# Decode attention of two blocks on one core: the first load, block A's wq, as eight loads of 16 rows

## The chip, the core and the metric

The kernel runs on one core of a Trainium2 chip. The metric is device time in microseconds (us) of one execution. Before the change the median of three runs is 1937.3 us (1937.21 to 1937.73). One further execution was taken with the hardware profiler; its page and trace are what is read here.

## What is computed

Two blocks, A and B, each one decoding step of attention: a batch of 2, one query position, 32 heads of 192, a cache of 8192 positions. A projects x with wq to a query for each head, takes the softmax of its products with the cached keys, sums the cached values by it and projects with wo; B does the same with its own data. All data is bfloat16.

```
def _A_ref(x, k_cache, v_cache, wq, wo):
    q = (x @ wq).reshape(B, Sq, Hq, Dh).transpose(0, 2, 1, 3)
    scores = jnp.einsum("bhqd,bhkd->bhqk", q, k) * (Dh ** -0.5)
    p = _softmax(scores, axis=-1)
    o = jnp.einsum("bhqk,bhkd->bhqd", p, v)
    return o.transpose(0, 2, 1, 3).reshape(B, Sq, Hq * Dh) @ wo
...
return jnp.concatenate([a, b], axis=-1)
```

The caches are 4 x 201 MB, each wq and wo 7.9 MB (640 x 6144 and 6144 x 640). Every byte is read once.

## The kernel before

**Units.** The work is cut into 64 units: 2 blocks x 16 pairs of heads x 2 batch entries. A unit has one k load and one v load, each 128 rows (partitions) of 24576 elements: two heads, 64 rows to a head. Three buffers of that size (`NBUF` = 3) lie in one large tile, `big`; loads take them in turn. Block A's wq and block B's wq (128 rows of 30720 elements each, `WQE`) lie at first where buffers 1 and 2 and the product tiles will be.

**Engines.** For a unit, VectorE (DVE) multiplies k by the query in four chunks (L285), TensorE (PE) sums the products over groups of elements with an identity matrix (L362), DVE reduces these to scores (L289) and takes the maximum, GpSimd (POOL) spreads the maximum over all partitions (L266), ScalarE (ACT) takes the exponential (L324), and PE multiplies it with v (L376). The result is divided by its sum and kept in `qall` for the last projection.

**The prologue.** PE waits for x (the semaphore `("x",)`), transposes it (`pe_x`, L345), and DVE spreads it over partitions (L271). Then PE waits for block A's wq, and makes the queries of block A's 16 pairs (L354); then it waits for block B's wq, and makes those of block B. DVE (L275) and ACT (L280) copy them into `qall`. The first product L285 waits for all of them.

**Loads.** All are issued on one queue, by the SyncE engine (SP), in an order written out by hand (L480 to L492): wq A, x A, x B, wq B, then k and v of all units, then wo A, and wo B in five pieces of 29, 11, 5, 2 and 1 rows of wo for each partition, and the two stores of the output. A k or v load waits before its issue for the work that last read its buffer (`done`); the second and third of them wait for the queries of block A and of block B. wq A is issued ahead of the stream's list and has no wait.

**Semaphores of loads.** Each load adds 16 to a semaphore when it is complete. `dsem(k, n)` makes one for key `k`, and whoever waits for the key waits for 16 times `n`. The two loads of x share one with `n` = 2.

**The tail.** PE multiplies the collected outputs with wo, 96 products for each block (L404); block B's start when its first piece has landed. ACT and DVE copy the result out of the accumulator, and SP stores it.

Of the kernel before, what the change touches and what calls it, by code (L numbers as in the profile page):

```python
# [117 lines left out]
def build_kernel(nc, blocks, out):  # L118
# [28 lines left out]
    with ExitStack() as es:  # L147
# [7 lines left out]
        big = sb("big", [128, NBUF * BUFE + 2 * PRODE], BF16)  # L155
# [28 lines left out]
        WQE = DC * Hn * Dh  # L184
        wq_off = [BUFE, BUFE + WQE]
# [10 lines left out]
        S_act = _Stream("act", sem("s_act"), reg)  # L196
        S_dve = _Stream("dve", sem("s_dve"), reg)
        S_pool = _Stream("pool", sem("s_pool"), reg)
        bsem = [sem(f"bsem{i}") for i in range(NBUF)]

        def dsem(k, n=1):
            reg[k] = (sem("d_" + "_".join(str(i) for i in k)), 16 * n)

        dsem(("x",), NBLK)
        for blk in range(NBLK):
            dsem(("wq", blk))
            dsem(("odone", blk))

        loads = [("k", 0)]
# [14 lines left out]
        for blk, rows, off, w in ((0, (WR,), woA, [("s", LASTU, NCH - 1)]), (1, (29,), wo0, [("pv", LASTU - 1)]),  # L224
                                  (1, (11, 5, 2, 1), wo1, [("pv", LASTU)])):
            r = 29 if off == wo1 else 0
            for n in rows:
                pieces.append((blk, r, r + n, off, w))
                off, r, w = off + n * D, r + n, []
# [13 lines left out]
        def dma(out_ap, in_ap, k):  # L243
            s = reg[k][0]
            return lambda eng: eng.dma_start(out_ap, in_ap).then_inc(s, 16)  # L245
# [1 line left out]
        def ld_x(blk):  # L247
            return dma(x4[B * blk:B * blk + B, :], blocks[blk]["x"][:, 0, :], ("x",))

        def ld_wq(blk):  # L250
            src = blocks[blk]["wq"].rearrange("(j c) n -> j (c n)", c=DC)
            return dma(big[:, wq_off[blk]:wq_off[blk] + WQE], src, ("wq", blk))

        def ld_wo(n):
            blk, r0, r1, off, _ = pieces[n]
# [218 lines left out]
        def done(i):  # L474
# [2 lines left out]
            kind, u = loads[i]  # L477
            return ("m", u, NCH - 1) if kind == "k" else ("pv", u)

        ld_wq(0)(nc.sync)  # L480
        for blk in range(NBLK):
            S_sp.add(ld_x(blk))
        S_sp.add(ld_wq(1))
        for i, (kind, u) in enumerate(loads):
            w = [done(i - NBUF)]
# [73 lines left out]
def bass_concat_heads__gqa_block_cached__mha_block_cached__decode_kernel(  # L559
    nc: bass.Bass,  # L560
    A_x: bass.AP,
    A_k_cache: bass.AP,
    A_v_cache: bass.AP,
    A_wq: bass.AP,
    A_wo: bass.AP,
    B_x: bass.AP,
    B_k_cache: bass.AP,
    B_v_cache: bass.AP,
    B_wq: bass.AP,
    B_wo: bass.AP,  # L570
    out: bass.AP,
):
    blocks = [
        dict(x=A_x, k=A_k_cache, v=A_v_cache, wq=A_wq, wo=A_wo),
        dict(x=B_x, k=B_k_cache, v=B_v_cache, wq=B_wq, wo=B_wo),
    ]
    build_kernel(nc, blocks, out)
# [28 lines left out]
```

## Time and profile before

| what | value |
|---|---|
| median of three runs | 1937.3 us (1937.21 to 1937.73) |
| the profiled execution's own time | 1937.8 us |
| its span, first to last instruction | 1936.3 us |
| PE, DVE, ACT, POOL busy | 1506.7, 1122.1, 143.1, 28.6 us |
| mean granted PE clock | 0.953 |
| read from device memory | 836.77 MB, 432 GB/s over the span |
| wq A, from issue to landing | 20.9 us |
| wq B, from issue to landing | 37.9 us |
| a k or v load, from issue to landing (median) | 27.6 to 29.3 us |
| PE's first wait, for x | until 21.41 us |
| PE's last 96 products (L404, block B) | start at 1926.17 us |

The times of the page count from the first instruction. Engines: SP's queue is named SPq, and a line of the timeline gives start, duration, engine, line, operation and the tile written and read. A row of the windows' view gives a stretch, its length, the busy time of PE, PE's weight loads, DVE, ACT and POOL (with the number of instructions that start in it), the granted PE clock, the mean busy share of the 16 transfer engines, and the rate. Packets of a transfer are counted in the stretch in which they start.

### The profile page before, as it was taken

How to read it: one execution, taken by the hardware profiler on the slowest of the kernel's cores; microseconds unless marked ns; L12 is line 12 of the kernel's file. 1: busy time of each engine (PE TensorE's matmuls, PEld its weight loads, DVE VectorE, ACT ScalarE, POOL GpSimd, SP SyncE). 2: the span in 40 equal slices, each digit the busy share in tenths (PEclk: the TensorE clock that was granted, in tenths of full speed). 3: DMA queues.
4: the chain of work that ended last, by engine and by line, in shares of the span. 5: the costliest groups of instructions: out<-in, count | busy, mean ns of one | idle time of the engine just before them, and what ended most of it. 6: DMA issues, size and time to landing. Idle time of an engine off the chain costs nothing.

```text
span 1936.3 us, 19044 instructions
## 1 busy us (share of the span) xinstructions
PE 1506.7 (78%) x7721; PEld 731.1 (38%) x7721; DVE 1122.1 (58%) x907; ACT 143.1 (7%) x519; POOL 28.6 (1%) x113
## 2 busy tenths in 40 slices
PE   4777877877877877877877877877878878878878
PEld 2333433333433333433333433433334434434434
DVE  4765565565565565565565565565565565565560
ACT  3100000000000000000000000000000000000000
POOL 0000000000000000000000000000000000000000
PEclk9899999999999999999999999999988988988988
DMA  9999999999999999999999999999999999999999
GB/s 419 428 433 439 431 434 436 433 434 434 438 431 433 438 431 435 435 435 432 435 438 431 434 436 434 432 435 439 430 434 437 432 434 435 436 431 435 438 430 388
DMA packets 19610, 836.91 MB, mean 432 GB/s; under 512 B 2184, under 2 KB 2320, under 8 KB 2576
## 3 DMA queue, kind: packets, MB, share of 16 engines
q1 hardware_dynamic: 19600, 836.78, 99.9%
q8 instruction: 6, 0.10, 0.0%
q14 instruction: 4, 0.03, 0.0%
HBM read 836.77 MB, written 0.01 MB: 432 GB/s over the span
## 4 chain that ended last, share of the span: by engine, by line
DMA 49%; PE 31%; DVE 16%; issue 3%; DVEq 0%; SPq 0%; ACT 0%; ACTq 0%
DMA big<-in_B_k_cache_dram 24%; DMA big<-in_A_k_cache_dram 22%; PE ops L376 17%; DVE big L285 15%; PE scps L362 12%; DMA big<-in_B_wq_dram 2%; DMA big<-in_B_wo_dram 1%; DVE sc L289 1%; PE scps L354 0%; PE scps L404 0%; PE ops L368 0%; PE outps L354 0%; DVEq L285 0%; DVE qall L275 0%; SPq L245 0%
## 5 line engine op out<-in xcount | busy, mean ns | idle before, releaser
L285 DVE TENSOR_TENSOR big<-big,qall 128x6144 bf16<-128x6144 bf16 x256 | 853.0, 3352 | 519.6 <-DMA big<-in_B_k_cache_dram 259.8
L362 PE MATMUL scps<-big,ident 128*128 128x512 bf16 x3072 | 778.4, 410 | 395.8 <-DVE big L285 393.5
L376 PE MATMUL ops<-big,pb 128*34 128x384 bf16 x4096 | 676.8, 326 | 0.0
L362 PEld LDWEIGHTS scps<-big,ident 128*128 128x128 bf16 x3072 | 302.4, 104 | 865.1 <-DVE big L285 486.1
L376 PEld LDWEIGHTS ops<-big,pb 128*34 128x34 bf16 x4096 | 395.5, 98 | 258.7
L289 DVE TENSOR_REDUCE sc<-scps 128x32 f32<-128x512 f32 x256 | 176.2, 688 | 201.2 <-PE scps L362 201.2
L315 ACT ACTIVATE nb<-mg 64x1 f32<-64x1 f32 x128 | 25.9, 202 | 1707.6 <-POOL mg L266 1706.8
L324 ACT ACTIVATE pb<-sc,nb 64x128 bf16<-64x128 f32 x128 | 56.1, 438 | 7.8
L266 POOL PARTITION_ALL_REDUCE mg<-mp x64 | 25.9, 404 | 1859.2 <-DVE mp L295 1859.2
L295 DVE TENSOR_REDUCE mp<-sc 64x1 f32<-64x128 f32 x128 | 35.9, 280 | 8.3
L309 ACT ACTIVATE qall<-o_sum,rc 2x192 f32 (+1 forms) x64 | 29.2, 456 | 20.6 <-DVE o_sum L306 19.1
L306 DVE TENSOR_TENSOR o_sum<-ops,o_hi 2x192 f32<-2x192 f32 x64 | 22.1, 346 | 7.7
L354 PE MATMUL scps<-big,xw 128*128 x120 | 23.2, 351 | 2.8 <-DVE xw L271 2.2
L324 ACT ACTIVATION_READ_ACCUMULATOR pb<-sc,nb 64x1 f32 x128 | 23.9, 187 | 0.0
L303 DVE COPY o_hi<-ops 2x192 f32<-2x192 f32 x64 | 22.3, 348 | 2.0
L300 DVE RECIPROCAL rc<-ops 2x1 f32<-2x1 f32 x64 | 9.9, 155 | 21.3 <-PE ops L376 19.4
L275 DVE CAST qall<-scps 64x192 f32 x48 | 17.0, 355 | 7.3 <-PE scps L354 5.6
L280 ACT ACTIVATE qall<-scps 64x192 f32 x48 | 15.7, 326 | 30.5 <-DVE qall L275 28.3
L345 PE MATMUL oTps<-ident,xw 4*128 4x4 bf16 x5 | 0.4, 178 | 21.4 <-DMA xw<-in_B_x_dram 21.4
L354 PEld LDWEIGHTS scps<-big,xw 128*128 128x128 bf16 x120 | 12.4, 103 | 12.2 <-issue 6.1
L368 PEld LDWEIGHTS ops<-ones,rs 128*2 128x2 f32 x128 | 5.5, 82 | 26.9 <-issue 26.9
L271 DVE CAST xw<-oTps 128x320 bf16<-128x320 f32 x4 | 1.7, 484 | 18.5 <-PE oTps L345 18.5
(34 smaller groups left out, 74.0 us busy)
## 6 DMA issues: line engine op xcount, KB each, us to landing
big<-in_A_k_cache_dram SPq DMA_DIRECT2D x32, 6144.0 KB, 29.3
big<-in_A_v_cache_dram SPq DMA_DIRECT2D x32, 6144.0 KB, 28.3
big<-in_B_k_cache_dram SPq DMA_DIRECT2D x32, 6144.0 KB, 28.6
big<-in_B_v_cache_dram SPq DMA_DIRECT2D x32, 6144.0 KB, 27.6
big<-in_A_wq_dram SPq DMA_DIRECT2D x1, 7680.0 KB, 20.9
big<-in_B_wq_dram SPq DMA_DIRECT2D x1, 7680.0 KB, 37.9
big<-in_A_wo_dram SPq DMA_DIRECT2D x1, 7680.0 KB, 28.7
big<-in_B_wo_dram SPq DMA_DIRECT2D x1, 4640.0 KB, 29.0
```

The lines of the kernel that those rows point to most:

```text
L266: return lambda eng: eng.partition_all_reduce(mg[u % 3][:], mp[u % 3][:], 128, bass.bass_isa.ReduceOp.max)
L285: return lambda eng: eng.tensor_tensor(prod[c % 2], t[:, c * TC:(c + 1) * TC, :], qall[:, S_dve.at(u), :].broadcast_to([128, TC, Dh]), ALU ...
L289: return lambda eng: eng.tensor_reduce(sc[u % 3][:, c * TC:(c + 1) * TC], scps[(u * NCH + c) % 3][:], AXL.X, ALU.add)
L295: ins = eng.tensor_reduce(mp[u % 3][r, s:s + 1], sc[u % 3][r, :], AXL.X, ALU.max)
L303: return lambda eng: eng.tensor_copy(o_hi[:], ops[u % 3][32:34, Dh:QW])
L306: return lambda eng: eng.tensor_tensor(o_sum[:], ops[u % 3][0:2, 0:Dh], o_hi[:], ALU.add)
L309: return lambda eng: eng.activation(qall[0:2, S_act.at(u), :], o_sum[:].unsqueeze(1), ACTF.Identity, scale=rc[u % 3][:])
L315: ins = eng.activation(nb[u % 3][r, :], mg[u % 3][r, s:s + 1], ACTF.Identity, scale=-scale)
L324: ins = eng.activation(dst, sc[u % 3][r, :].rearrange("p (g j a) -> p g a j", j=JB, a=2), ACTF.Exp, bias=nb[u % 3][r, :], scale=scale, acc ...
L354: ins = eng.matmul(qps[hp % NQ][:, 0:QW], xbc[:, blk, c, :], wq_t[blk][:, c, S_pe.at(off, QW, QW)], start=(c == 0), stop=(c == DC - 1))
L362: ins = eng.matmul(scps[(u * NCH + c) % 3][:], ident[:], prod[c % 2][:, :, j * DG:(j + 1) * DG], start=(j == 0), stop=(j == NJ - 1))
L376: ins = eng.matmul(ops[u % 3][0:MP, 0:QW], pb[u % 3][:, j0s:j0s + MP], vv[:, j, :], start=(j == 0), stop=(j == TJ - 1))
```

## The change

The load of block A's wq, 128 rows on 128 partitions, becomes eight loads on the same queue, one after the other. The r-th has rows r, r + 8, r + 16 and so on, 16 rows. Destination, source and bytes are the same. All eight add to the one semaphore, and its key is waited for at 128 in place of 16. `ld_wq` takes the rows as an argument; block B's wq is loaded as before. Two lines are added in all, so that later line numbers differ by one or two.

```
+        QR = 8
...
         for blk in range(NBLK):
-            dsem(("wq", blk))
+            dsem(("wq", blk), QR if blk == 0 else 1)
...
-        def ld_wq(blk):
+        def ld_wq(blk, rows=slice(None)):
             src = blocks[blk]["wq"].rearrange("(j c) n -> j (c n)", c=DC)
-            return dma(big[:, wq_off[blk]:wq_off[blk] + WQE], src, ("wq", blk))
+            return dma(big[rows, wq_off[blk]:wq_off[blk] + WQE], src[rows], ("wq", blk))
...
-        ld_wq(0)(nc.sync)
+        for r in range(QR):
+            ld_wq(0, slice(r, 128, QR))(nc.sync)
```

## The prediction

> **What bounds the kernel now.** I read the page's transfer rows first, then the chain that ended last, then the SP queue's timeline of the first microseconds, then windows cut finely around the first load, and last the windows of the tail. The page's second part and its third:
>
> ```profile
> DMA  9999999999999999999999999999999999999999
> GB/s 419 428 433 439 431 434 436 433 434 434 438 431 433 438 431 435 435 435 432 435 438 431 434 436 434 432 435 439 430 434 437 432 434 435 436 431 435 438 430 388
> DMA packets 19610, 836.91 MB, mean 432 GB/s; under 512 B 2184, under 2 KB 2320, under 8 KB 2576
> ...
> q1 hardware_dynamic: 19600, 836.78, 99.9%
> ...
> DMA 49%; PE 31%; DVE 16%; issue 3%; DVEq 0%; SPq 0%; ACT 0%; ACTq 0%
> ```
>
> All 40 slices have the transfer engines at 90% or more, the one queue fills 99.9% of them, and the rate stands at 430 to 439 GB/s from the third slice to the last but one. The chain gives only 49% to DMA, but that is because it follows a buffer from landing through DVE and PE to the next issue. While it does so, another load is already moving. So time is bytes over rate: 836.78 MB at 434 GB/s is 1928.1 us. The span has 1936.3; what is left, 8.2 us, lies at the two ends, in slices 1, 2 and 40. The change touches the first end alone.
>
> SP's queue in the first 3 us (start, duration, what):
>
> ```profile
> 0.72 0.40 SPq L245 DMA_DIRECT2D big<-in_A_wq_dram  x1
> 1.18 0.31 SPq L245 DMA_DIRECT2D xw<-in_A_x_dram  x1
> 1.54 0.23 SPq L245 DMA_DIRECT2D xw<-in_B_x_dram  x1
> 1.81 0.36 SPq L245 DMA_DIRECT2D big<-in_B_wq_dram  x1
> 2.21 0.71 SPq L245 DMA_DIRECT2D big<-in_A_k_cache_dram  x1
> ```
>
> An issue takes 0.23 to 0.71 us, nearly the same for 2 rows as for 128, and the five are out by 2.9 us, while the first load lands at 0.72 + 20.9 = 21.6 us (the page's table of issues). Now the windows around its first and second rows (window, its length, five engines, PE clock, DMA share, GB/s). In this view a packet counts with all its bytes and time in the window in which it starts, which is why a share can exceed 1:
>
> ```profile
> 1.50:2.00 0.50, 0.00 (x0) 0.00 (x0) 0.00 (x0) 0.50 (x1) 0.50 (x18) 1.00 3.51 1106
> 2.00:2.50 0.50, 0.00 (x0) 0.00 (x0) 0.40 (x3) 0.41 (x3) 0.50 (x9) 1.00 1.43 492
> 2.50:3.00 0.50, 0.00 (x0) 0.00 (x0) 0.45 (x3) 0.00 (x0) 0.50 (x5) 1.00 1.00 369
> 3.00:3.50 0.50, 0.00 (x0) 0.00 (x0) 0.27 (x1) 0.00 (x0) 0.25 (x1) 1.00 0.00 0
> 4.00:5.00 1.00, 0.00 (x0) 0.00 (x0) 0.00 (x0) 0.00 (x0) 0.00 (x0) 1.00 1.13 492
> 4.60:4.80 0.20, 0.00 (x0) 0.00 (x0) 0.00 (x0) 0.00 (x0) 0.00 (x0) 1.00 1.42 614
> ...
> 5.40:5.60 0.20, 0.00 (x0) 0.00 (x0) 0.00 (x0) 0.00 (x0) 0.00 (x0) 1.00 1.42 614
> 5.60:5.80 0.20, 0.00 (x0) 0.00 (x0) 0.00 (x0) 0.00 (x0) 0.00 (x0) 1.00 0.00 0
> ```
>
> A row of wq is 30720 bf16 = 61.44 KB. 1106 GB/s over 0.50 us is 553 KB, nine rows; then four, then three: 16 rows, one for each engine, and the engines set off over some 1.0 us (the finer windows put five of them in 1.70:1.80 and the last one in 2.70:2.90). The nine took 3.51 x 0.50 x 16 / 9 = 3.12 us each, the four 2.86, the three 2.67. Eight of the second rows start in 4.00:5.00 (492 KB) and take 1.13 x 1.00 x 16 / 8 = 2.26 us, which is the pace kept from there on; the other eight follow by 5.6 us. So the first row costs the last engine about 5.5 us from the span's start, and that stagger of 0.8 us is still there when wq A lands (5.5 + 7 x 2.26 = 21.3).
>
> The tail:
>
> ```profile
> 1926.00:1928.00 2.00, 1.83 (x18) 1.03 (x20) 0.00 (x0) 0.00 (x0) 0.00 (x0) 0.65 0.99 422
> 1928.00:1930.00 2.00, 2.00 (x18) 0.94 (x15) 0.00 (x0) 0.00 (x0) 0.00 (x0) 0.50 0.99 413
> 1930.00:1932.00 2.00, 2.00 (x32) 1.32 (x30) 0.00 (x0) 0.00 (x0) 0.00 (x0) 1.00 0.86 341
> ```
>
> Transfers run until about 1932; PE's last 96 products (L404, from 1926.17) start when block B's first wo piece lands. A transfer stream that is ahead by x arrives there ahead by x.
>
> **The change, part by part.** Removed: one load of 128 rows. Added: eight loads of 16 rows, all rows the same 61.44 KB, so bytes and large packets stay. The loads go out in the same place, before the first x, and what follows on every engine is the same instructions.
>
> *Issues.* Seven more. The spacing of issues above is 0.27 to 0.46 us, so 7 x 0.27 = 1.9 to 7 x 0.46 = 3.2 us. SP's queue behind them is x A, x B, wq B and block A's first k load, which move from 1.18, 1.54, 1.81 and 2.21 to between 3.1 and 5.4. Who waits: PE for x (L345), which starts at 21.41. What hides it: wq A's own eight rows on every engine, until 4.6 + 7 x 2.26 = 20.4 us on the earliest. That leaves 15 us, so I cost it at nothing. Without the cover it would be the 1.9 to 3.2 us in full. Inside wq A: the second 16-row load is issued at about 1.1, its rows are wanted at about 4; the r-th has 2.26 us more each time and needs 0.46. Nothing.
>
> *Closing packets.* The page's 2184 packets under 512 B are 16 for each of 136 loads of 128 rows and 2 for each of the four of two rows. Seven more loads make 112 more, 7 per engine. No row prices one alone. From below: nothing. From above: from 100 to 200 us the windows give 433 GB/s with a load's end about every 14.5 us, while bare rows move 16 x 61.44 KB in 2.26 us, 435; so an end costs at most 0.5% of 14.5, 0.07 us, and seven cost 0.5. I take 0.05 us, near the lower end: the windows' own rounding of 2.26 is as large as that difference.
>
> *The start of the engines, the term that decides.* First packet now: issue at 0.72, first rows at 1.75, 1.03 us later. The last load of the kernel, out of two rows, is issued at 1935.1 and its first packet comes in 1935.80:1935.85, 0.75 later. A 16-row load lies between: 1.50 to 1.75; I take 1.75, since a k load's issue takes hardly longer than x's. The stagger of 1.0 us: if it is the time to hand out 128 rows in order (the last engine's first row is row 120), it is 8 ns a row, and 16 rows need 0.13 us; if it has nothing to do with rows it stays 1.0. I take 0.13, because the next rows, already handed out, follow without a break. The excess of a first row over 2.26 is 3.12 - 2.26 = 0.86 for the nine that set off close together and 0.41 for the last three. Now all 16 set off together, so I take 0.86; bounds 0 and 0.86. Last engine through its first row: 1.75 + 0.13 + 2.26 + 0.86 = 5.0, against 5.5: gain 0.5. Bounds: 1.50 + 0.13 + 2.26 = 3.9, gain 1.6; 1.75 + 1.0 + 2.26 + 0.86 = 5.9, loss 0.4.
>
> *To the end.* Queued loads keep the engines busy (issue to landing 28 to 29 us for 14.5 us of transfer), so 0.5 less 0.05 = 0.45 us arrives at the tail. There PE's clock was 0.50 for about 3.4 us (0.65 in the first window, 0.50 in the second): 18 products in 2.00 us, against 32 at 1.00. A second such stretch would cost 3.4 x (32 - 18) / 32 = 1.5 us. I take none, and keep it for the upper end.
>
> *Sum.* Span 1936.3 - 0.45 = 1935.85; this execution took 1937.8, 1.5 us around the span and 0.5 above the median of the runs, 1937.3. The same step on the median: 1936.85, said as 1936.9.
>
> [...]
>
> **The rivals.**
> *Nothing gained.* The first rows are late because all engines start cold, and the stagger is theirs, not the order's. For it: even rows that set off alone took 2.67 on average. Against it: the last starters took least. Time: 1937.3 + 0.05, up to 1937.7 with the loss of 0.4.
> *All of it gained.* With one descriptor each, stagger and excess both go: 1937.3 - 1.6 + 0.05 = 1935.7. For it: 0.41 excess for the late starters; against it: 0.86 for the close ones. Faster than this by much it can't be: the bound of 2.26 us a row is untouched.
> *A restart at each 16-row load* (slower). Each load's rows begin only when the load before has closed, and each time the 1.03 us from issue to first packet is paid: 7 x 1.03 = 7.2 us, 1944.5. Place: between the first and ninth row of every engine; from 0.56 us a load (3.9 / 7) it decides the verdict. Half of it, 0.86 us of first-row excess each time because the engines set off in step, is 6.0 us, 1943.3, the same mechanism by the nearer row. For it: the 1.03 is what an idle queue shows. Against it: x A, x B and wq B were queued behind wq A, and the window 20.00:22.00, in which the one load ends and the next begins, has 494 GB/s, 16 rows in 2 us like its neighbours.
> *It doesn't do what it says.* If 16 rows reached only eight engines, two each, wq A would take 36 us instead of 18 and the end would come 18 us later, 1955. Against it: 128 rows set off one to each of 16.
>
> **How the numbers follow.** The forecast 0.55, nothing gained 0.25, all gained 0.13; restart or excess at each load 0.05, eight engines 0.01, and 0.01 that the whole stream runs otherwise in my favour. A measurement of this kernel can tell about 0.2%, 3.9 us, from no change; forecast and the first two rivals lie inside, so same 0.93, slower 0.06, faster 0.01. The range goes from all gained, 1935.7, with 0.2 of spread between runs, to nothing gained with half the tail's clock stretch, 1937.5 + 0.8: 1935.5 to 1938.3. Only the slower rivals are left out.
>
> **What would show it.** Changed profile: eight issues ahead of x's, about 0.3 to 0.46 us apart, the k load's issue before 5.5 us; packets 19722, 2296 of them under 512 B; 16 rows starting within 0.2 us of 1.75; the last second row before 5.2 us; wq A landing near 21.1; 433 GB/s in the middle. Wrong if second rows start past 5.6 (nothing gained), before 4.2 (all gained), if an engine's rows between 4 and 20 us start more than 2.26 us apart, so that wq A lands after 22 (restart), or if L404's last start moves against wq A's landing.

## The result

The changed kernel is slower: median 1956.87 us (1956.65 to 1957.64, five runs) against 1937.3 (1936.99 to 1937.73, five runs of the kernel before beside them). The ratio is 1.0101, 95% interval 1.009 to 1.0113, so 19.6 us more. The forecast was 1936.9, with a range up to 1938.3.

The page of the changed kernel, transfers and chain (its span is 1955.4 us, its own time 1956.87):

```profile
DMA  9999999999999999999999999999999999999999
GB/s 241 434 432 434 434 435 433 433 434 434 434 433 434 434 433 433 433 433 432 432 434 434 434 433 434 434 433 434 434 434 433 434 434 434 434 434 434 434 433 392
DMA packets 19722, 836.91 MB, mean 428 GB/s; under 512 B 2296, under 2 KB 2432, under 8 KB 2688
...
DMA 49%; PE 28%; DVE 17%; issue 5%; SPq 0%; DVEq 0%; ACT 0%; ACTq 0%
```

Only the first slice has changed clearly: 241 GB/s in place of 419. The engines' busy share is still 90% or more there. The packets are the ones that were counted out ahead (19722, 2296 of them small). Share and rate part here: with 90% or more busy in both, the first slice moved 419 GB/s before and 241 now. The rate is what tells.

SP's queue at the start (start, duration, what):

```profile
0.72 5.04 SPq L246 DMA_DIRECT2D big<-in_A_wq_dram  x8
5.80 0.48 SPq L246 DMA_DIRECT2D xw<-in_A_x_dram  x1
6.33 0.24 SPq L246 DMA_DIRECT2D xw<-in_B_x_dram  x1
6.61 0.36 SPq L246 DMA_DIRECT2D big<-in_B_wq_dram  x1
7.02 53.53 SPq L246 DMA_DIRECT2D big<-in_A_k_cache_dram  x2
```

The eight issues take 0.63 us each, more than was allowed for, but the last of the four loads behind them is out at 7.45 (7.02 and 0.43), and wq B's first row starts only at 39.67. The issues are covered, as forecast. (The last line holds two k loads; the second waits for its buffer.)

Windows of the changed kernel, with the columns of before (window, length, PE, PE's loads, DVE, ACT, POOL, PE clock, DMA share, GB/s):

```profile
2.00:2.50 0.50, 0.00 (x0) 0.00 (x0) 0.41 (x3) 0.41 (x3) 0.50 (x8) 1.00 7.09 1475
2.50:3.00 0.50, 0.00 (x0) 0.00 (x0) 0.45 (x3) 0.00 (x0) 0.50 (x5) 1.00 1.66 369
3.00:3.50 0.50, 0.00 (x0) 0.00 (x0) 0.26 (x1) 0.00 (x0) 0.24 (x1) 1.00 0.57 123
3.50:6.40 2.90, 0.00 (x0) 0.00 (x0) 0.00 (x0) 0.00 (x0) 0.00 (x0) 1.00 0.00 0
6.40:7.80 1.40, 0.00 (x0) 0.00 (x0) 0.00 (x0) 0.00 (x0) 0.00 (x0) 1.00 3.42 702
...
6.45:39.67 33.22, 0.00 (x0) 0.00 (x0) 0.00 (x0) 0.00 (x0) 0.00 (x0) 1.00 1.00 207
```

Twelve rows start in the first window (1475 x 0.50 / 61.44), three in the next, one in the third: 16 rows, one for each engine, and the engines' mean share from the second rows on is 1.00. The 12 of the first window take 7.09 x 0.50 x 16 / 12 = 4.7 us each, where 3.12 stood before. The 16 second rows start in 6.40:7.80, and from there to the first row of wq B (6.45:39.67, 112 rows) a row takes 33.22 x 16 / 112 = 4.75 us. The same stretch in the kernel before, also 112 rows:

```profile
4.69:20.55 15.86, 0.00 (x0) 0.00 (x0) 0.00 (x0) 0.00 (x0) 0.00 (x0) 1.00 1.00 434
```

2.27 us a row. The account: 33.22 - 15.86 = 17.4 us in rows two to eight, 6.45 - 4.69 = 1.8 before the second rows start; 19.1 together, which is the difference of the spans (1955.4 - 1936.3 = 19.1). Nothing was lost or won back later. (The medians differ by 19.6, because the profiled execution before took 1937.8, 0.5 above its median.) wq A's rows move at 207 GB/s in place of 434, all the time that they last.

### The profile page after: what moved, and what is told of

Read it like the earlier page. It is cut to its first block, busy times and chain, and to the rows that moved or that the text cites. A ratio compares the mean times of both kernels' runs of the same rounds, so it can differ in the third digit from the quotient of the medians.

```text
span 1955.4 us, 19051 instructions
## 1 busy us (share of the span) xinstructions
PE 1507.9 (77%) x7721; PEld 732.1 (37%) x7721; DVE 1123.0 (57%) x907; ACT 142.4 (7%) x519; POOL 28.6 (1%) x113
## 2 busy tenths in 40 slices
DMA packets 19722, 836.91 MB, mean 428 GB/s; under 512 B 2296, under 2 KB 2432, under 8 KB 2688
## 4 chain that ended last, share of the span: by engine, by line
DMA 49%; PE 28%; DVE 17%; issue 5%; SPq 0%; DVEq 0%; ACT 0%; ACTq 0%
DMA big<-in_B_k_cache_dram 24%; DMA big<-in_A_k_cache_dram 22%; PE ops L377 18%; DVE big L286 15%; PE scps L363 9%; DVE sc L290 2%; DMA xw<-in_B_x_dram 2%; DMA big<-in_B_wo_dram 1%; PE scps L355 1%; PE outps L355 0%; SPq L246 0%; PE ops L369 0%; DVEq L286 0%; DVE qall L276 0%; PE scps L405 0%
## 5 line engine op out<-in xcount | busy, mean ns | idle before, releaser
L310 ACT ACTIVATE qall<-o_sum,rc 2x192 f32 (+1 forms) x64 | 29.0, 453 | 20.7 <-DVE o_sum L307 19.1
L307 DVE TENSOR_TENSOR o_sum<-ops,o_hi 2x192 f32<-2x192 f32 x64 | 22.1, 345 | 7.7
## 6 DMA issues: line engine op xcount, KB each, us to landing
big<-in_A_wq_dram SPq DMA_DIRECT2D x8, 960.0 KB, 22.1
```

The costliest lines, as they stand in the source:

```text
L307: return lambda eng: eng.tensor_tensor(o_sum[:], ops[u % 3][0:2, 0:Dh], o_hi[:], ALU.add)
L310: return lambda eng: eng.activation(qall[0:2, S_act.at(u), :], o_sum[:].unsqueeze(1), ACTF.Identity, scale=rc[u % 3][:])
```

## The experiments

Theories A, B, C, E and F are told in the expectations as they came up, theory D after the run of four loads. Each edit is shown against the changed kernel.

**Sixteen neighbouring rows to a load.**

```
-            ld_wq(0, slice(r, 128, QR))(nc.sync)
+            ld_wq(0, slice(16 * r, 16 * r + 16))(nc.sync)
```

> Eight loads of 16 rows stay, but each has 16 neighbouring rows (0 to 15, 16 to 31, ...) in place of every eighth. In the changed kernel a row of wq A took 2.39 x 2.00 x 16 / 16 = 4.78 us (window 6.00:8.00, 16 rows) against 2.26 before. Theory A (source): 16 rows that are read at the same time from places 8 rows = 492 KB apart go at half pace; then this kernel is near 1937 (1936.3 to 1938.0) and its rows take 2.26 us. Theory B (destination): writes to partitions 8 apart at the same time go at half pace; also near 1937. Theory C (small loads): a load that gives each engine one row goes at half pace whatever its rows; then 1956 to 1958 and rows of 4.78 us.

Measured: 1988.24 us (four runs), ratio to before 1.0262, interval 1.0245 to 1.0279. None of the three had this. The stretch from the first second row to wq B:

```profile
9.12:70.23 61.11, 0.00 (x0) 0.00 (x0) 0.00 (x0) 0.00 (x0) 0.00 (x0) 1.00 1.00 113
```

113 GB/s, 61.11 x 16 / 112 = 8.73 us a row. So which rows stand together in a load does matter, and here closer is worse. Theory C falls. A and B had expected the opposite of what happened; whether it is the source or the destination stays open.

**Source and destination apart.** `ld_wq` takes the source's rows as an argument of their own; first the step is on the source only, then on the destination only:

```
-            ld_wq(0, slice(r, 128, QR))(nc.sync)
+            ld_wq(0, slice(16 * r, 16 * r + 16), slice(r, 128, QR))(nc.sync)
```

> As the kernel before it, with 16 neighbouring partitions as destination, but every eighth row of wq A as source; so rows of wq A land on other partitions than x is laid out for, and block A's queries are others. A: 1956 to 1958. B: near 1937. C: 1956 to 1958.

```
-            ld_wq(0, slice(r, 128, QR))(nc.sync)
+            ld_wq(0, slice(r, 128, QR), slice(16 * r, 16 * r + 16))(nc.sync)
```

> The other half: every eighth partition as destination, 16 neighbouring rows of wq A as source; block A's queries are others here too. A: near 1937. B: 1956 to 1958. C: 1956 to 1958.

Measured: 1986.98 us with neighbouring destinations, 1957.46 with stepped destinations (one run each). The same stretch of each, in this order:

```profile
8.61:69.27 60.66, 0.00 (x0) 0.00 (x0) 0.00 (x0) 0.00 (x0) 0.00 (x0) 1.00 1.00 113
6.40:39.60 33.20, 0.00 (x0) 0.00 (x0) 0.00 (x0) 0.00 (x0) 0.00 (x0) 1.00 1.00 207
```

Each has the rate of the kernel with the same destinations, and its time to 1.3 and 0.6 us. Where the rows come from in device memory makes no difference to the rate that shows (113 and 113, 207 and 207 GB/s). Theory A falls. It is the destination, though not by B's idea of steps of 8.

**Four loads of 32 rows, every fourth row.**

```
-        QR = 8
+        QR = 4
```

> Four loads of 32 rows, every fourth row in turn. If in a load each engine has a run of its rows (two here), the same 16 rows are read together as in the changed kernel, and A and B say 1956 to 1958 again, or, if they mind the distance of rows in the load alone (4 rows, 246 KB), something from 1937 to 1958; C says less than the changed kernel, since half as many rows stand at a load's start, about 1947.

Measured: 1937.9 us (one run), the time of before. C's 1947 misses it, and so do the 1956 to 1958 of A and B; their weaker form, anything from 1937 to 1958, left it open. The stretch from the first second row to wq B:

```profile
4.99:20.88 15.89, 0.00 (x0) 0.00 (x0) 0.00 (x0) 0.00 (x0) 0.00 (x0) 1.00 1.00 433
```

That is the pace of before, 434. The rates 113, 207 and 433 stand about as 4 to 8 to 16, and theory D supposes from that: the 128 partitions fall into 16 groups, as many as there are engines, and a group takes in about 434 / 16 = 27 GB/s, a row of wq in 2.27 us, which the rows of a load that are in one group share. Sixteen neighbours then reach 4 groups, every eighth partition 8, every fourth of all 128 all 16. Which partitions make up a group three rates do not fix: how many groups D gives each of the kernels that follow was the author's estimate, and the kernels test it.

**The number of loads by itself**, with all partitions in each:

```
-            ld_wq(0, slice(r, 128, QR))(nc.sync)
+            ld_wq(0, r * WQE // QR, (r + 1) * WQE // QR)(nc.sync)
```

(`ld_wq` here takes the first and last column.)

> Eight loads of the same 960 KB each, but cut along the columns: all 128 partitions, an eighth of each row. The destination decides by the four runs so far; what is left to say is what eight loads cost when each reaches all partitions. [...] By D this kernel is at 1936.9 to 1938.2. Theory F: a load for itself costs, and the eight closings are a part of the 19.6 us: 1940 or more.

Measured: 1937.33 us (ten runs) against 1937.42 (13), ratio 1.0, interval 0.999 to 1.001. D holds, F falls: what eight loads with their closing packets cost is lost in the 0.1%, 2 us, that the interval leaves.

**Three ways to reach eight groups.** 32 neighbours to a load; 16 rows by step 2; 16 rows by step 4:

```
+        QR = 4
...
+            ld_wq(0, slice(32 * r, 32 * r + 32))(nc.sync)
```

> Four loads of 32 rows as the four by every fourth row that came out at 1937.9, but each with 32 neighbouring partitions. D: 32 neighbours lie in 8 of the 16 groups, so half pace, wq A about 18 us longer: 1955 to 1958. Theory E: what hurts is one row per engine in a load, the more the closer the partitions (16 neighbours 1988, every eighth 1957), and two rows per engine mend it: 1937 to 1938.

```
+            b = 32 * (r // 2) + r % 2
+            ld_wq(0, slice(b, b + 32 - r % 2, 2))(nc.sync)
```

> Eight loads of 16 rows, every second row of a run of 32. D: 8 groups, two rows in each, as in the changed kernel: 1955 to 1958. E: between every eighth (1957) and neighbours (1988), by halving of distances about 1977.

```
+            b = 64 * (r // 4) + r % 4
+            ld_wq(0, slice(b, b + 64 - r % 4, 4))(nc.sync)
```

> Eight loads of 16 rows, every fourth row of a run of 64. D: 8 groups, two rows in each: 1955 to 1958. E: about 1967.

Measured: 1956.27, 1956.79 and 1956.37 us (one run each); 206, 205 and 210 GB/s. The lines of the first and the third:

```profile
6.14:39.56 33.42, 0.00 (x0) 0.00 (x0) 0.00 (x0) 0.00 (x0) 0.00 (x0) 1.00 1.00 206
6.31:39.15 32.84, 0.00 (x0) 0.00 (x0) 0.00 (x0) 0.00 (x0) 0.00 (x0) 1.00 1.00 210
```

All three are D's, half of the 434 within 6%. Theory E, by distance and rows for each engine, misses all three. The run of 64 by step 4 says which halves count: if partitions 32 apart were in different groups, it would have reached 16 and run at full pace.

Taken together the runs say this of the groups, if rows of one group share its pace. Sixteen neighbours run at about a quarter of 434 (113), so they reach 4 groups; which of the sixteen are together in one no run shows. Rows 4 apart in a run of 32 are in different groups: in the last experiment below, eight of them at a time take 2.3 us each. Partitions 32 apart add no group (a run of 64 by step 4, 210), and partitions 64 apart do (every fourth of all 128, 433).

| load of wq A | groups it reaches, by D | GB/s | time, us |
|---|---|---|---|
| one of 128 rows (before) | 16 | 434 | 1937.3 |
| 32 rows by 4 (the second run is timed below) | 16 | 433; 429 | 1937.9; 1937.66 |
| 16 rows by 8 (the change) | 8 | 207 | 1956.87 |
| 16 rows by 2; by 4 | 8 | 205; 210 | 1956.79; 1956.37 |
| 32 neighbours | 8 | 206 | 1956.27 |
| 16 neighbours | 4 | 113 | 1988.24 |

At 434 / 16 GB/s to a group, 8 and 4 groups would make 217 and 109 GB/s, an estimate from the window of the kernel before; the windows have 205 to 210 and 113, within 6% of it.

**Another order of the same eight loads.**

```
-        for r in range(QR):
+        for r in (0, 4, 1, 5, 2, 6, 3, 7):
             ld_wq(0, slice(r, 128, QR))(nc.sync)
```

> The same eight loads of every eighth row, issued in the order 0, 4, 1, 5, 2, 6, 3, 7. [...] D: faster than the changed kernel, wq A shorter by 2 to 10 us, 1947 to 1955. If a load is slow in itself, whatever else is in flight: 1956 to 1957.7 as in the old order.

Measured: 1955.85 us (1955.28 to 1956.36, four runs), ratio to before 1.0093, interval 1.0078 to 1.0109. That lies between both expectations and misses both: about 1 us below the changed kernel, whose lowest run is 1956.65.

```profile
6.55:38.62 32.07, 0.00 (x0) 0.00 (x0) 0.00 (x0) 0.00 (x0) 0.00 (x0) 1.00 1.00 215
```

A row takes 32.07 x 16 / 112 = 4.58 us, near twice 2.27. The 1947 to 1955 was the author's estimate: that loads next to each other in this order have no group in common, and that an engine ahead of the one it shares a group with goes on into a free group. The second is not shown, and the first only in part: loads 0 and 4 together have the partitions of one load by 4, which ran at 433, so by the rates those two share no group; of loads 4 and 1 no run says it.

**Block B's wq in eight loads, block A's in one.**

```
-            dsem(("wq", blk), QR if blk == 0 else 1)
+            dsem(("wq", blk), QR if blk == 1 else 1)
...
-        for r in range(QR):
-            ld_wq(0, slice(r, 128, QR))(nc.sync)
+        ld_wq(0)(nc.sync)
...
-        S_sp.add(ld_wq(1))
+        for r in range(QR):
+            S_sp.add(ld_wq(1, slice(r, 128, QR)))
```

> Block A's wq is one load again; block B's, which is queued behind it, becomes the eight loads. D: the pace is lost wherever such loads stand in the queue, 1956 to 1958, with wq A landed at 21.6 as before. If the loss needs the start of the kernel (empty queue, engines that set out together): near 1938.

Measured: 1957.81 us (one run). wq A landed 22.1 us after its issue, where 20.9 had been expected. The stretch in which wq B moves, while PE, DVE and ACT make block A's queries:

```profile
24.60:57.90 33.30, 14.47 (x80) 8.16 (x78) 11.35 (x32) 10.41 (x32) 0.00 (x0) 0.75 1.00 207
```

The same 207 GB/s in the middle of the queue, behind a load that ran at its pace of before (393 GB/s in 8.00:18.00 in both kernels). The loss does not need the empty queue at the start.

**Four loads of 32 rows, timed.** The edit is that of the four loads above (`QR = 4`).

> The four loads of 32 rows, every fourth row in turn, again, now timed, to see whether a split that reaches all 16 groups gains or loses at the start. In its one profile SP's four issues took 2.54 us, and the first rows set out from 2.1 us on, later than the 1.75 of before; the theory of the groups asks for the pace of before otherwise. D: 1937.5 to 1938.3, 0.1 to 0.9 us slower than before. If the split gains at the start as was predicted: 1936.5 to 1937.1.

Measured: 1937.66 us (1937.32 to 1938.54, 11 runs) against 1937.39 (1937.09 to 1938.07, 15 runs), ratio 1.0001, interval 0.9992 to 1.001. No difference that can be told. The gain of 0.45 us that was predicted would be too small for this interval, but the profiles show no sign of it: wq B's rows begin at 20.88 and 20.89 us in the two profiles of this kernel, against 20.55 before, and PE's wait for x ends at 22.0 us in the first of them, against 21.41.

**Sixteen loads of 8 rows, each with a group to itself.**

```
-        QR = 8
+        QR = 16
...
+            b = 32 * (r // 4) + r % 4
+            ld_wq(0, slice(b, b + 32 - r % 4, 4))(nc.sync)
```

> Sixteen loads of 8 rows, every fourth row of a run of 32, so that each of a load's rows has a group of its own, and still one row for an engine in a load. D: a row that has its group to itself takes 2.26 us again; but a load then reaches 8 groups with 8 engines, so the rate is that of half the engines, 217 GB/s, and wq A takes 16 x 2.26 = 36.2 us plus the start: 1955 to 1957, the same time as the changed kernel from rows of half the duration. If a load with one row for an engine is slow in itself, rows of 4.5 us or more: 16 x 4.5 = 72, 1990 or more. If eight rows are spread over 16 engines in some other way, two loads can be in flight at once and it comes out below 1950.

Measured: 1975.78 us (one run), outside what was expected. Three stretches:

```profile
5.00:14.00 9.00, 0.00 (x0) 0.00 (x0) 0.00 (x0) 0.00 (x0) 0.00 (x0) 1.00 0.51 218
14.00:21.00 7.00, 0.00 (x0) 0.00 (x0) 0.00 (x0) 0.00 (x0) 0.00 (x0) 1.00 1.05 421
23.00:44.00 21.00, 0.00 (x0) 0.00 (x0) 0.00 (x0) 0.00 (x0) 0.00 (x0) 1.00 0.89 190
```

In the first, half the engines are busy (0.51), and 32 rows (218 x 9 / 61.44) take 0.51 x 9 x 16 / 32 = 2.3 us each. A load with one row for an engine is not slow in itself: these rows, which have a group each by D, take 2.3 us, against 2.27 in the kernel before. In the second stretch, with wq B issued at 12.37, the share is 1.05 and the rate 421 GB/s: all 16 run, and the other half is taken to be at wq B, the next large load on the queue. In the third, 65 rows take 0.89 x 21 x 16 / 65 = 4.6 us. Loads 1 to 8 go to partitions 0 to 63, loads 9 to 16 to 64 to 127; the ninth begins at about 21.1 us, an estimate (first rows at 2.1 us as in the changed kernel, 0.86 us longer than the others as in the kernel before, and 8 x 2.27). By D it then meets wq B's rows in the groups of that half, and this is what the expectation had left out. That reading fits the moment of the change, but was not tested by itself.

## Why the prediction was wrong

*The step that failed* is in "The change, part by part": "all rows the same 61.44 KB, so bytes and large packets stay". Bytes and packets did stay, but from them the sum kept the pace as well: 2.26 us a row for all eight rows of an engine (7 x 2.26 in "Issues"), and in the second rival "the bound of 2.26 us a row is untouched". The 2.26 us was read from a load of 128 rows and taken as the pace of a transfer engine. By the runs it holds where, by D, each engine's row has a group of partitions to itself: 2.27 us in the load of 128 rows, 2.3 in the loads of 8. The change, by D, gives 16 engines 8 groups; a row then took 4.75 us, and rows two to eight alone took 17.4 us more (33.22 against 15.86). That the destination of a load could set its pace was no step of the sum and no rival.

*The forecast's gain at the start* did not come either. I took 0.13 us for the stagger of the first rows, on the idea that it is the time to hand out 128 rows. With 16 rows it is still 1.0 us: the first six rows start in 2.10:2.20 (3686 GB/s there), the last one in 3.10:3.20 (614). The other bound, 1.0 us "if it has nothing to do with rows", was right. That the last engine starts with row 120 is shown by no view. The first rows of the change set out after 2.10, outside the bounds of 1.50 to 1.75. Where all partitions, or every fourth of them, are in each load, the split gained nothing that shows: 1937.33 and 1937.66, the rival "nothing gained".

*Closing packets* were counted right, 112 more. Their price of 0.05 us was neither confirmed nor refuted: the eight loads of columns put all that seven more loads cost within 0.1%, 2 us, of nothing.

*Issues*: 0.63 us each, not 0.27 to 0.46, and the first k load went out at 7.02 instead of before 5.5. The cover of 15 us held all the same.

*To the end*: all of the loss arrived at the end, as it was said that a gain would (19.1 us where wq B's rows begin, 39.67 against 20.55, and 19.1 in the span).

*The rivals.* "A restart at each 16-row load" said 1944.5 and 1943.3; the loss is about three times that, as a steady 4.75 us a row with no pause between loads (a share of 1.00), so its mechanism is not what happened. "If 16 rows reached only eight engines" said 1955, near the time, because half the engines and half the groups make the same arithmetic. That nearness is luck: the windows show 16 rows at once and a share of 1.00, where eight engines would show about half (0.51 with the loads of 8 rows): by D half of the *groups* were reached, not half of the engines.

## What to carry to other kernels

Before a load is split by partitions, look at which partitions each piece writes at a time: here pieces of 16 partitions by 8, 4 or 2 and of 32 neighbours moved at 205 to 210 GB/s, 16 neighbours at 113, where the whole load had 434; whether the rows came from neighbouring or spread places of device memory made no difference (207 and 207, 113 and 113). Splitting along the columns (1937.33 us), or by every fourth partition over all 128 (1937.66), kept the time of before (1937.3). In a stage bound by transfers read the rate and not the busy share: at 207 and at 113 GB/s the share was 1.00, as at 434.

## What the runs showed of the hardware

- The destination's partitions set the pace of the load of wq: 113 GB/s for 16 neighbours, 207 for 16 by 8, 434 for all 128. With the 4, 8 and 16 groups of theory D that is 28, 26 and 27 GB/s to a group, not quite constant. What makes the rows of the change 4.75 us rather than twice 2.27, and 4.58 in another order, stays open.
- In these runs a stepped destination came with longer issues and, where a window shows it, a later first packet. Eight issues took 5.04 us in the changed kernel and with the step on the destination alone, 5.21 and 5.22 with steps of 4 and 2, but 4.06 for neighbours and 3.89 with the step on the source alone. With runs of 32 neighbours, rows set out in 1.50:2.00 (1352 GB/s there); with 16 rows by step 2 or 4, none before 2.00, and by 8, none before 2.10.
